# Attention followed by a two-layer MLP: the first two batches as quads of heads, in one written order

## The chip, the cores and the metric

The kernel runs on one core of a Trainium2 chip. The metric is the time of one execution in microseconds (us); a verdict compares the median of several executions of two kernels on the same chip. A profile is of one execution, and its times count from the first instruction of the program (its span).

The engines are PE (TensorE, matrix products, with the weight loads PEld), ACT (ScalarE), DVE (VectorE), POOL (GpSimd) and SP (SyncE). Each works through its own queue in order, and they wait for one another by semaphores. PE writes into PSUM, from where ACT and DVE read. DMAs are issued from the queues of SP, ACT and POOL.

## The reference: what is computed

For each of 8 batches and 12 heads (448 tokens, head size 64):

```python
scores = scale * np.matmul(q, k.transpose(0, 1, 3, 2))
m = np.max(scores, axis=-1, keepdims=True)
e = np.exp(scores - m)
attn = e / (np.sum(e, axis=-1, keepdims=True) + np.exp(-m) + 1e-09)
x = np.matmul(attn, v)          # then [B * S, H * D] = 3584 x 768
h = x @ w_in                    # 768 x 2048
g = np.maximum(h, 0.0) ** 2
out = g @ w_out                 # 2048 x 768
```

The kernel leaves the maximum out: exp(s) / (sum of exp(s) + 1) is the same quotient.

## The kernel before: tiles, stages and the order of the work

**Attention.** Scores are made transposed: keys on the partitions, queries along the columns. So the exponentials (ACT, L222) can go straight into the next product as its moving operand, and the row sums are a product with a tile of ones. The quotient is taken as exp(-ln(sum)) on ACT (L290 and L291), and DVE multiplies it in while it moves the values' product out of PSUM (L299, L302).

Batches 0 and 1 are worked on as *pairs* of heads. `load_natural` puts every fourth token on 112 partitions. `transposes` (L206) makes q and k of two heads of 64 rows each, one above the other. `scores` (L231) then runs two 64 x 112 tiles beside each other on PE (64 rows, 112 columns); `values` (L269) and `row_sums` (L276) run two 112 x 64 tiles. Before the row sums DVE adds the four key chunks up (`add_chunks`, L248).

Batches 2 to 7 are worked on as *quads* of heads: 64 keys at a time, in four 64 x 64 tiles of PE side by side (`visit` L317, `values_quad` L381, `sums_quad` L364). Batch 2 has its q and k transposed on PE (`transposes_quad`, L184); from batch 3 on a DMA does it (`stage`, `transposed_loads`).

**MLP.** `tile_in` (L435) makes 128 of the 2048 hidden features for a stretch of tokens: six products over the 768 inputs, each as two 128 x 64 tiles beside each other (`product`, L419 in mode COLS2). `relu_squared` (L425) takes ReLU and square. `tile_out` (L478) makes 128 tokens x 384 outputs out of 16 products (L491).

**The order.** The instructions of an engine run as they are written. For batch 0 the pairs are units of 192 queries (i = 0 to 5) and then of 256 queries (6 to 11), for batch 1 units of 448 (12 to 17). In the loops from L625 on each unit's scores, sums and values are written with a lag of one or two units, and between them `drain` (L573) puts in as much of the first layer as a share of its estimated time says:

```python
        scores(u, et, 0)
        for at in transpose_at.get(i, ()):
            transposes(*at)
        drain(share[0] * (1.2 if first else 0.45))
        scores(u, et, 1)
        ...
            rcp = row_sums(done, (ess.pop(i - 1)[0:1],))
            values(prev, ets.pop(i - 1), xp)
        drain(share[0] * 0.15)
```

Warm-up matmuls (`keep_warm`, L590) stand at the very start (9) and between the first units (6 more). From L779 on the batches from 2 on run in a steady loop: `between` puts 11 score steps of the quads between products of the second layer or of values, then 16 `tile_in` of the batch before follow, and so on. The first call of `between`, with 11 steps of batch 2 and three `tile_out` of batch 0, comes ahead of the first layer of batch 1.

**Loads** all go through POOL's queue (L520 to L535), in f16, except for the first three pairs of batch 0, which SP and ACT load as they are, in f32, to be cast. Behind batch 0 the queue has half of win, batch 1's first three pairs, the other half of win, batch 1's rest. A load into a buffer that is still read waits for PE.

**PSUM.** `s_psum` has two tiles of [128, 2, 512] for scores, `x_psum` one of [128, 512] and `m_psum` three, for the values, sums, transposes and the MLP. From batch 0's second layer on every fourth such tile is taken from `x_psum`, so that four take turns (`mp_tile`, L403).

Of the kernel before, what the change touches and what calls it, by code (L numbers as in the profile page):

```python
# [16 lines left out]
def kernel(  # L17
# [14 lines left out]
    NPAIR = H // 2  # L32
# [3 lines left out]
    P = S // RUN  # L36
    NQ = H // 4
    KC = S // 64
    PAIRED = (0, 1)
    ON_PE = (0, 1, 2)  # L40
    COLS = H * S // 2 + 16
    HALF = DM // 2

    scale = 1.0 / float(D) ** 0.5
    GS = 256.0
    OUT_SCALE = 1.0 / (GS * GS)

# [14 lines left out]
    x_psum = ctx.enter_context(tc.tile_pool(name="x_psum", bufs=1, space=bass.MemoryType.PSUM))  # L62
    m_psum = ctx.enter_context(tc.tile_pool(name="m_psum", bufs=3, space=bass.MemoryType.PSUM))
# [9 lines left out]
    q_r = q.rearrange("b h (p t) d -> b p h t d", t=RUN)  # L73
    k_r = k.rearrange("b h (p t) d -> b p h t d", t=RUN)
    v_r = v.rearrange("b h (p t) d -> b p h t d", t=RUN)
    win_r = moe_w_in.rearrange("(c p) f -> p c f", p=128)
    wout_r = moe_w_out.rearrange("(c p) f -> p c f", p=128)

    whole, vns, qks, xts, naturals, stages = {}, {}, {}, {}, {}, {}

    def quads_of(t, t0, n, run):

        return t[:, :, t0:t0 + n * run].rearrange("b (i x) (p t) d -> b i p x (t d)", i=2, t=run)

    def load_v_quads(b):
        vn = vns[b] = v_pool.tile([128, NQ, 2, KC, D], FP16, name="vn")
        for i in range(2):
            rows_ = vn[64 * i:64 * i + 64].rearrange("p g j c d -> p (g j) (c d)")
            parts = ((0, KC),) if b in ON_PE else ((0, KC - 1), (KC - 1, KC))
            for c0, c1 in parts:  # L90
                nc.gpsimd.dma_start(out=rows_[:, :, c0 * D:c1 * D], in_=quads_of(v, 64 * c0, 64, c1 - c0)[b, i])

    def load_natural_quads(b, g0, g1):
        t = nat.tile([128, RUN * 2 * S], FP16, name=f"nn{0 if g0 == 0 else 1}")
        w = 2 * S
        for n, r in enumerate((q, k)):
            part = t[:, n * (g1 - g0) * w:(n + 1) * (g1 - g0) * w].rearrange("p (h x) -> p h x", x=S)
            for i in range(2):
                nc.gpsimd.dma_start(out=part[64 * i:64 * i + 64], in_=quads_of(r, 0, 64, KC)[b, i][:, 2 * g0:2 * g1])
            for g in range(g0, g1):  # L100
                naturals["qk"[n], b, "quad", g] = part[:, 2 * (g - g0):2 * (g - g0) + 2].rearrange(
                    "p j (c d) -> p j c d", d=D)

    def load_v(b, p0, p1):
        hs = slice(2 * p0, 2 * p1)
        if b not in vns:
            vns[b] = v_pool.tile([P, H, RUN, D], FP16, name="vn")
        nc.gpsimd.dma_start(out=vns[b][:, hs], in_=v_r[b, :, hs])

    def load_natural(b, p0, p1):  # L110

        raw = b == 0 and p1 <= 3
        for n, r in (("q", q_r), ("k", k_r)):
            src = r[b, :, 2 * p0:2 * p1]
            if raw:
                if p0 == 0:
                    whole[n] = e_pool.tile([P, RUN * S], FP32, name="et")
                t = whole[n][:, p0 * 512:(p0 + 1) * 512].rearrange("p (h t d) -> p h t d", h=2, t=RUN)
                (nc.sync if n == "q" else nc.scalar).dma_start(out=t, in_=src)
            else:  # L120
                if p0 % 3 == 0 and n == "q":
                    whole["both"] = nat.tile([P, RUN * 2 * S], FP16, name=f"nn{p0 // 3}")
                w = NPAIR * RUN * D
                t = whole["both"][:, w * (n == "k"):w * (n == "k") + w].rearrange("p (h t d) -> p h t d", t=RUN, d=D)
                t = t[:, 2 * (p0 % 3):2 * (p0 % 3 + p1 - p0)]
                nc.gpsimd.dma_start(out=t, in_=src)
            for pr in range(p0, p1):
                naturals[n, b, pr] = t[:, 2 * (pr - p0):2 * (pr - p0) + 2]

    def load_win(i, n):  # L130
        w = DF // n
        nc.gpsimd.dma_start(out=win[:, :, i * w:(i + 1) * w], in_=win_r[:, :, i * w:(i + 1) * w])
# [4 lines left out]

# [30 lines left out]

# [13 lines left out]
    def transposes_quad(b, g):  # L184
        if b not in qks:
            qks[b] = qk_pool.tile([128, 3, COLS], FP16, name="qk")
        for n in range(2):
            tp = mp_tile(FP16).rearrange("p a x -> p (a x)")
            for c in range(KC):
                for j in range(2):  # L190
                    nc.tensor.transpose(tp[64 * j:64 * j + 64, 128 * c:128 * c + 128],
                                        naturals["qk"[n], b, "quad", g][:, j, c, :], ident)
            nc.vector.tensor_copy(  # L193
                qks[b][:, n, 2 * S * g:2 * S * (g + 1)].rearrange("p (i c x) -> p c i x", i=2, c=KC),
                tp[:, 0:2 * S].rearrange("p (c i x) -> p c i x", c=KC, i=2))

    def cast(b, pr):
        for name in "qk":
            f = flat.tile([P, 2, RUN, D], FP16, name=f"flat{name}")
            if pr < 2 and name == "k":  # L200
                nc.scalar.activation(out=f, in_=naturals[name, b, pr], func=AF.Copy)
            else:
                nc.vector.tensor_copy(f, naturals[name, b, pr])
            naturals[name, b, pr] = f

    def transposes(b, pr):  # L206
        tp = mp_tile(FP16)
        for i, name in enumerate("qk"):
            for s in range(RUN):
                for h in range(2):  # L210
                    nc.tensor.transpose(tp[64 * h:64 * h + 64, i, P * s:P * s + P],  # L211
                                        naturals[name, b, pr][:, h, s, :], ident[0:P, 0:P])
        if b not in qks:
            qks[b] = qk_pool.tile([128, 3, COLS], FP16, name="qk")
        parts = (0, S // 2, S) if b == 0 and pr < 3 else (0, S)
        for x, y in zip(parts, parts[1:]):
            nc.vector.tensor_copy(qks[b][:, 0:2, pr * S + x:pr * S + y], tp[:, :, x:y])

# [3 lines left out]
    def chunk(et, u, c, kk):  # L224

        n = u[3]
        if n < S:
            return et[:, 0:RUN * 2 * n].rearrange("p (c h j n) -> p c h j n", c=2, h=2, j=2)[:, c, :, kk % 2, :]
        return et.rearrange("p (k x) -> p k x", k=RUN)[:, kk]

    def scores(u, et, c, only=(0, 1)):  # L231
        b, pr, q0, n = u
        qk = qks[b]
        two = [] if n == S else s_psum.tile([P, 2, 512], FP32, name="sp")
        for kk in [2 * c + x for x in only]:
            sp = s_psum.tile([P, 2, 512], FP32, name="sp") if n == S else two
            o = 0 if n == S else kk % 2 * n
            for h in range(2):
                r = slice(64 * h, 64 * h + 64)
# [22 lines left out]
    def of_head(e, u, h):  # L262

        b, _, _, n = u
        if n < S:
            return e[:, h]
# [587 lines left out]
```

## Time and profile before

| | us |
|---|---|
| median of 3 runs | 407.46 (407.33 to 408.98) |
| span of the profiled execution | 405.9 |
| PE busy | 394.9 (97%) |
| DVE busy | 277.2 (68%) |
| ACT busy | 224.1 (55%) |
| first product of batch 1's first layer (L419, 448 columns) starts at | 81.60 |

How to read it: a row of a timeline gives the start, the time from the first start to the last end, the engine, the line, the operation, the tiles written and read, their shape and their number; in brackets the idle time before it and who ended it. Matmuls overlap, so the distance between the starts of two rows says what the first cost. For PE "64*112" are the rows and columns of the array that a matmul uses. In a landing row the last number is the time from issue to landing in us, and KB are those written.

### The profile page before, as it was taken

What the parts mean: (1) busy time and instruction counts of PE and PEld (TensorE: products, weight loads), DVE (VectorE), ACT (ScalarE), POOL (GpSimd) and SP (SyncE); (2) the same over time, 40 slices, a digit from 0 to 9 for tenths busy, and PEclk for the clock granted to TensorE, in tenths of its full rate; (3) what the DMA queues carried; (4) which work ended last, traced back from release to release, by engine and by line L of the source; (5) the groups of instructions that cost most, each with busy time, mean ns of one, the idle gap of its engine ahead of it and who ended that gap; (6) DMA issues with size and microseconds to landing.
All of it is one profiled execution on the core that took longest, in us unless ns stands there. A gap on an engine that the chain in (4) does not pass through costs nothing.

```text
span 405.9 us, 14479 instructions
## 1 busy us (share of the span) xinstructions
PE 394.9 (97%) x6627; PEld 262.4 (65%) x6627; DVE 277.2 (68%) x507; ACT 224.1 (55%) x277; POOL 59.5 (15%) x93
## 2 busy tenths in 40 slices
PE   7899998999999999999999999999999999999997
PEld 3567676667676666757666675757666675555664
DVE  3778888786967867686967867686967868186000
ACT  4898986928465564836466473836466473100111
POOL 6524140005000320003200440005000000000000
PEclk9999999999999999999999999999999999999999
DMA  9999999498706794186925694186501020100222
GB/s 186 197 197 198 203 204 208 105 196 113 175 3 126 122 186 102 42 134 144 189 69 129 119 191 95 42 155 122 120 3 40 3 80 4 48 31 0 79 78 79
DMA packets 77118, 45.83 MB, mean 113 GB/s; under 512 B 46720, under 2 KB 71552, under 8 KB 77056
## 3 DMA queue, kind: packets, MB, share of 16 engines
q0 software_dynamic: 30128, 22.16, 36.5%
q1 hardware_dynamic: 46208, 22.05, 24.5%
q8 instruction: 52, 0.85, 0.9%
q10 hardware_dynamic: 720, 0.69, 0.7%
q14 instruction: 10, 0.08, 0.1%
HBM read 45.69 MB, written 17.93 MB: 157 GB/s over the span
## 4 chain that ended last, share of the span: by engine, by line
PE 87%; DVE 5%; ACT 3%; DMA 2%; issue 1%; ACTq 0%; DVEq 0%
PE mp L491 26%; PE mp L419 22%; PE mp L421 10%; PE xp L419 6%; PE mp L390 6%; PE sp L346 5%; PE xp L421 4%; ACT et L222 2%; DMA et<-in_k_dram 2%; PE sp L241 2%; PE xp L273 2%; PE sp L332 1%; PE mp L211 1%; PE xp L491 1%; PE sp L375 1%
## 5 line engine op out<-in xcount | busy, mean ns | idle before, releaser
L222 ACT ACTIVATE et<-sp 128x896 f16<-128x896 f32 (+3 forms) x132 | 118.0, 915 | 26.0 <-PE sp L346 13.0
L491 PE MATMUL mp<-wout,gs 64*64 64x384 f16 x1760 | 125.6, 323 | 0.0
L419 PEld LDWEIGHTS <-win 128*64 128x64 f16 x1536 | 85.0, 110 | 47.7 <-issue 7.2
L419 PE MATMUL mp<-xt,win 128*64 128x448 f16 (+2 forms) x1248 | 109.0, 324 | 2.2 <-DVE qk L193 1.3
L491 PEld LDWEIGHTS <-gs 64*64 64x64 f16 x2624 | 76.2, 107 | 23.0 <-issue 0.6
L491 PE MATMUL xp<-wout,gs 64*64 64x384 f16 x864 | 84.7, 323 | 0.0
L431 DVE TENSOR_SCALAR rt<-mp 128x448 f16<-128x448 f32 (+2 forms) x82 | 51.0, 622 | 19.0 <-PE mp L419 8.4
L433 DVE TENSOR_TENSOR gs<-rt 128x448 f16<-128x448 f16 (+2 forms) x128 | 50.4, 395 | 12.0 <-ACT rt L429 7.9
L222 ACT ACTIVATE nn<-sp 128x896 f16<-128x896 f32 x42 | 37.6, 913 | 14.0 <-PE sp L346 12.3
L429 ACT ACTIVATE rt<-mp 128x448 f16<-128x448 f32 x18 | 9.8, 543 | 60.0 <-PE mp L419 48.3
L498 DVE TENSOR_SCALAR ot<-mp 128x384 f32<-128x384 f32 x41 | 22.7, 554 | 27.3 <-PE xp L491 19.9
L181 POOL COPY flatq<-qk 64x384 f16<-64x384 f16 x20 | 13.6, 704 | 186.9 <-DMA qk<-stage_k 186.6
L421 PEld LDWEIGHTS <-gs 128*128 128x128 f16 x256 | 24.4, 98 | 15.1 <-issue 0.4
L346 PE MATMUL sp<-qk 64*64 64x224 f16 x720 | 32.9, 258 | 0.0
L419 PE MATMUL xp<-xt,win 128*64 128x448 f16 x288 | 31.3, 352 | 0.0
L421 PE MATMUL mp<-wout,gs 128*128 128x384 f16 (+2 forms) x192 | 29.6, 313 | 0.0
L346 PEld LDWEIGHTS <-qk 64*64 64x64 f16 x720 | 22.4, 119 | 10.7 <-issue 3.6
L500 ACT ACTIVATE ot<-mp 128x384 f32<-128x384 f32 (+2 forms) x12 | 5.6, 463 | 42.4 <-PE mp L421 42.4
L396 DVE TENSOR_TENSOR xt<-mp,rcp 128x448 f16<-128x448 f32 x34 | 19.7, 619 | 8.2 <-PE mp L390 7.8
L378 ACT ACTIVATE rcp<-sp,one_b 128x896 f32<-128x896 f32 x18 | 18.1, 1003 | 6.3 <-PE sp L371 6.3
L390 PEld LDWEIGHTS <-vn 64*64 64x64 f16 x504 | 14.4, 107 | 6.1 <-issue 0.4
L390 PE MATMUL mp<-et,vn 64*64 64x448 f16 x308 | 18.3, 349 | 0.0
(82 smaller groups left out, 392.6 us busy)
## 6 DMA issues: line engine op xcount, KB each, us to landing
out_dram<-ot SPq DMA_DIRECT2D x9, 384.0 KB, 2.3
win<-in_moe_w_in_dram POOLq DMA_DIRECT2D x8, 384.0 KB, 14.0
wout<-in_moe_w_out_dram POOLq DMA_DIRECT2D x4, 768.0 KB, 17.8
vn<-in_v_dram POOLq DMA_DIRECT2D x10, 288.0 KB, 5.4
out_dram<-ot SPq DMA_DIRECT2D x15, 192.0 KB, 3.0
stage_q<-in_q_dram POOLq DMA_DIRECT2D x4, 676.0 KB, 9.8
stage_k<-in_k_dram POOLq DMA_DIRECT2D x4, 676.0 KB, 12.3
out_dram<-ot SPq DMA_DIRECT2D x7, 288.0 KB, 6.0
```

Source lines behind the costliest of these rows:

```text
L181: nc.gpsimd.tensor_copy(km[rows_].rearrange("p h (x o) -> p h x o", o=2)[:, :, :, odd], src[:, :, S // 2 - 32:S // 2])
L222: nc.scalar.activation(out=out_, in_=in_, func=AF.Exp, scale=scale)
L346: nc.tensor.matmul(sp[64 * i:64 * i + 64, o, j * n:(j + 1) * n], keys, qk[r, 0, h * n:(h + 1) * n], start=True, stop=True)
L378: nc.scalar.activation(out=rcp, in_=zp[:, :, 0:S], func=AF.Ln, bias=one_b)
L390: nc.tensor.matmul(xps[i][64 * j:64 * j + 64, 0:S], vns[b][r, g, j, c, :], of_column(e[r], m, j), start=(c == 0), stop=(c == KC - 1))
L396: nc.vector.tensor_mul(xts[b][:, NQ * i + g, :], xps[i][:, 0:S], zqs[m][:, i, :])
L419: nc.tensor.matmul(out_[x:x + 64], lhsT[:, x:x + 64], rhs, start=start, stop=stop)
L421: nc.tensor.matmul(out_, lhsT, rhs, start=start, stop=stop)
L431: nc.vector.tensor_scalar(out=rt[:, 0:m], in0=hp[:, 0:m], scalar1=0.0, scalar2=None, op0=ALU.max)
L433: nc.vector.tensor_mul(gs[:, f0:f0 + per, t0 % RING:t0 % RING + n], r, r)
L491: nc.tensor.matmul(o[y:y + 64, 0:w], g[x:x + 64, y:y + 64], wout[x:x + 64, fb, n0:n0 + w], start=(fb == 0), stop=(fb == NFFB - 1))
L498: nc.vector.tensor_scalar(out=ot[:, n0:n0 + w], in0=op[:, 0:w], scalar1=OUT_SCALE, scalar2=None, op0=ALU.mult)
```

## The change

The pairs and all functions that serve them go (`load_v`, `load_natural`, `cast`, `transposes`, `scores`, `add_chunks`, `values`, `row_sums`, `normalise`, `drain`, `tiles_in_early` and the loops over units). Batches 0 and 1 become quads in 64 x 64 tiles, with 64 partitions for each of two heads. Heads 4g to 4g + 3 are quad g; so win's rows and the order of heads in the later batches change too, without other instructions.

Batch 0 is done in two halves of 224 queries (`half_scores`, `half_exp`). `post` makes values and row sums of a piece together, chunk by chunk on PE, into one pair of PSUM tiles. Half of batch 0's first layer (features 0 to 1023) is made for each half of the tokens (`half_in`), the other half of the features in 64 x 64 tiles over all tokens (`Square`). A square's two PSUM tiles are written by the upper rows of the array and by the lower rows in turn; where they swap, a no-op on SP's queue stands between (`after`).

Everything up to the transposes of batch 2's third quad is in one written order, ORDER, a list of steps. The letters: W warm-up, c cast, t and u transposes and copy of the first quad, T and U those of a quad (b, g, q or k), s scores, e exponentials, p `post`, z and x reciprocal and normalising of a half, i `half_in`, r and g its ReLU and square, q R G the same of a square, a adds, S and Z row sums and reciprocal of a quad, v and X its values and normalising, L loads, P the change of pools, o and O second layer. s, e and p 0 to 23 are pieces of batch 0; s and e 24 to 44 are batch 1's seven chunks of three quads, 45 to 55 those of batch 2. The last number of c, u, r and R says whether ACT does it (1) or DVE (0).

```diff
-    x_psum = ctx.enter_context(tc.tile_pool(name="x_psum", bufs=1, space=bass.MemoryType.PSUM))
-    m_psum = ctx.enter_context(tc.tile_pool(name="m_psum", bufs=3, space=bass.MemoryType.PSUM))
+    begin_psum = ExitStack()
+    x_psum = begin_psum.enter_context(tc.tile_pool(name="x_psum", bufs=1, space=bass.MemoryType.PSUM))
+    m_psum = begin_psum.enter_context(tc.tile_pool(name="m_psum", bufs=2, space=bass.MemoryType.PSUM))
...
+    def xp_pair():
+        return x_psum.tile([128, 2, 512], FP32, name="xp")
...
+    def load_first_quad():
+        raw = e_pool.tile([128, RUN * S], FP32, name="et")[:, 0:2 * S].rearrange("p (n x) -> p n x", n=2)
+        for c0, c1 in ((0, 4 * D), (4 * D, S)):
+            nc.sync.dma_start(out=raw[:, 0, c0:c1], in_=by_pairs["q"][0, :, 0, c0:c1])
+            nc.scalar.dma_start(out=raw[:, 1, c0:c1], in_=by_pairs["k"][0, :, 0, c0:c1])
...
+    def half_scores(at):
...
+        for x in range(2):
+            for o in range(2):
+                if x < len(two[o]):
+                    c, j = two[o][x]
+                    r = slice(64 * j, 64 * j + 64)
+                    for i in range(2):
+                        s0 = (2 * g + i) * S
+                        mm(sp[64 * i:64 * i + 64, o, x * FIRST:(x + 1) * FIRST], qk[r, 1, s0 + 64 * c:s0 + 64 * c + 64],
+                           qk[r, 0, s0 + q0:s0 + q0 + FIRST], start=True, stop=True)
...
+    def post(at):
...
+        for is_sum in range(2):
+            for c, j in todo:
+                for i in range(2):
+                    r = slice(64 * i, 64 * i + 64)
+                    key = (g, half, i, j)
+                    mm(xz[64 * j:64 * j + 64, i, is_sum * FIRST:(is_sum + 1) * FIRST],
+                       ones[r] if is_sum else vns[0][r, j, g, c, :], e[r, j, c], start=key not in opened,
+                       stop=bool(is_sum) and c == KC - 1)
...
+    class Square:
...
+        def part(self, flip, c0, c1):
...
+            for dc in range(c0, c1):
+                self.done += 1
+                for o in range(2):
+                    r = (o + flip) % 2
+                    rows_ = slice(64 * r, 64 * r + 64)
+                    for y in (0, 64):
+                        f = (self.f0 + o) * 128 + y
+                        got = mm(hp[o][y:y + 64, 0:S], win[rows_, dc, f:f + 64], xt[rows_, dc, :],
+                                 start=self.done == 1, stop=self.done == 2 * DCH)
+                        if self.last:
+                            after(got, self.last)
+                            self.last = None
+            if self.done == DCH:
+                self.last = nc.sync.nop()
+                after(self.last, got)
...
-    for pr in range(3):
-        load_natural(0, pr, pr + 1)
+    raw = load_first_quad()
...
-    load_v(0, 0, 3)
-    load_natural(0, 3, 4)
-    load_natural(0, 4, 6)
-    load_v(0, 3, 6)
-    for i in range(4):
-        load_win(i, 8)
-    load_natural(1, 0, 3)
-    for i in range(4, 8):
-        load_win(i, 8)
-    load_natural(1, 3, 6)
-    load_v(1, 0, 6)
+    load_first_second()
+    nat0 = nat.tile([128, RUN * 2 * S], FP16, name="nn0")
+    load_natural_quads(0, (1, 2), 0, nat0)
+    for g in range(NQ):
+        load_v_quads(0, g, g + 1)
+    NW = 4
+    for i in range(NW):
+        load_win(i, NW)
+    load_natural_quads(1, (0,), 0, nat.tile([128, RUN * 2 * S], FP16, name="nn1"))
+    load_v_quads(1)
+    load_natural_quads(1, (1, 2), 0, nat.tile([128, RUN * 2 * S], FP16, name="nn0"))
...
+    def other_ring():
+        begin_psum.close()
+        ring.append(ctx.enter_context(tc.tile_pool(name="ring", bufs=4, space=bass.MemoryType.PSUM)))
...
+    ORDER = """
+        W9 c0,0,0 c1,0,0 t0,0,0 c1,4,1 c0,4,0 t1,0,0 u0,0,0,0 u1,0,0,0 t1,0,4 t0,0,4 u1,0,4,1 s0 u0,0,4,0 t1,1,0
+        u1,1,0,0 t0,1,0 s1 u0,1,0,0 t0,1,4 e0 t1,1,4 u0,1,4,0 e1 u1,1,4,0 s2 T0,1,1 T0,1,0 U0,1,1 s3 T0,2,0 e2
+        e3 U0,1,0 s4 T0,2,1 s5 e4 U0,2,0 p0 s6 p1 e5 e6 s7 e7 p2 p3 U0,2,1 s8 z0 s9 e8 x0 e9 p4 s10 p5 s11 e10
+        p6 p7 s12 e11 z1 e12 s13 x1 p8 s14 e13 p9 e14 s15 e15 p10 p11 s16 s17 z2 x2 e16 p12 s18 p13 e17 e18 s19
+        p14 s20 p15 e19 z3 i0,3 i0,0 x3 r0,3,0 e20 p16 s21 r0,0,1 p17 s22 p18 T1,0,0 g0,3 e21 g0,0 e22 U1,0,0
+        p19 s23 T1,0,1 i0,1 U1,0,1 z4 s24 x4 e23 s25 e24 p20 p21 s26 e25 e26 p22 r0,1,0 s27 p23 z5 T1,1,0 g0,1
+        U1,1,0 i0,2 x5 s28 T1,1,1 r0,2,1 i1,1 e28 U1,1,1 L0 g0,2 e27 i1,0 r1,1,1 s29 r1,0,1 g1,1 s30 T1,2,1 a0,0
+        g1,0 U1,2,1 e29 i1,2 s31 e30 a0,1 a0,2 r1,2,1 s32 g1,2 P0 T2,1,0 e32 e31 a0,3 i1,3 T1,2,0 L1 s33 U2,1,0
+        r1,3,1 U1,2,0 q1,0,0,3 e33 s34 v0,0 g1,3 q1,0,3,6 e34 S0 v0,1 q1,1,0,3 v0,2 s35 v0,3 a1,0 q1,1,3,6 v0,4
+        v0,5 R1,0,0 Z0 s36 e35 R1,1,1 v0,6 G1,0 e36 s37 X0 T2,1,1 T2,0,0 e37 s38 T2,0,1 e38 U2,1,1 s39 q0,0,0,3
+        G1,1 s40 q0,0,3,6 e39 s41 U2,0,1 e40 U2,0,0 v1,0 q0,1,0,3 s42 a1,1 a1,2 e41 v1,1 a1,3 q0,1,3,6 v1,2 S1
+        R0,1,0 e42 v1,3 a2,0 R0,0,1 s43 v1,4 q2,0,0,3 Z1 v1,5 q2,0,3,6 v1,6 X1 s44 e43 G0,1 G0,0 q2,1,0,3 e44
+        s45 q2,1,3,6 e45 R2,0,0 q3,0,0,3 R2,1,1 s46 q3,0,3,6 s47 e46 e47 v2,0 q3,1,0,3 s48 v2,1 G2,1 G2,0
+        q3,1,3,6 v2,2 e48 s49 a2,1 v2,3 R3,0,0 e49 R3,1,0 s50 G3,1 o1,0,4 a2,2 s51 G3,0 a2,3 v2,4 e50 o1,4,8
+        v2,5 e51 s52 a3,0 S2 v2,6 e52 o2,0,4 o1,8,12 o2,4,8 a3,1 o1,12,16 Z2 X2 s53 e53 s54 o2,8,12 o0,0,4 a3,2
+        e54 a3,3 T2,2,0 O1 U2,2,0 S3 s55 o0,4,8 T2,2,1 o0,8,12 o2,12,16 U2,2,1 O2 e55 o0,12,16 Z3 O0
+    """
...
-    for i in range(NPAIR):
-        u, et, es, half = begin(i)
...
     complete(S)
+    del outs[0:EARLY]
...
     for b in range(2, B):
-        m = NQ * (b - 2)
-        n = min(3, len(outs))
-        ns = 12 * PIECE + n * TILE
-        work = second(n)
+        m = NQ * (b - 1)
         if b > 2:
-            ns += KC * PIECE
-            work = chain(timed(values_quad(m - 1)), work)
-        between([(m, c) for c in range(KC)] + [(m + 1, c) for c in range(4)], work, ns, {10: [m]})
-        if b == 2:
-            rcps = row_sums([units[-1]], (ess.pop(len(units) - 1)[0:1],))
-            xp = mp_tile()
-            values(units[-1], ets.pop(len(units) - 1), xp)
-            normalise([units[-1]], xp, rcps)
-            transposes_quad(2, 2)
+            n = min(3, len(outs))
+            ns = 12 * PIECE + n * TILE + KC * PIECE
+            work = chain(timed(values_quad(m - 1)), second(n))
+            between([(m, c) for c in range(KC)] + [(m + 1, c) for c in range(4)], work, ns, {10: [m]})
```

`load_first_second` loads the other two heads of the first quad, `load_natural_quads` q and k of the quads named, `load_v_quads` v, and `load_win` a quarter of win's columns in two DMAs of 64 partitions. L0 in ORDER issues batch 2's first two quads and wout, L1 the third quad, v and the copy of batch 3 for its transposing load.

## The prediction, made before the result was known

> **What bounds the kernel now.** I read the page first, then the window table, then the timelines of PE and ACT up to the place where the two kernels meet again, and last the issues of the loads. The page:
>
> ```profile
> PE 394.9 (97%) x6627; PEld 262.4 (65%) x6627; DVE 277.2 (68%) x507; ACT 224.1 (55%) x277; POOL 59.5 (15%) x93
> ...
> PE   7899998999999999999999999999999999999997
> ...
> ACT  4898986928465564836466473836466473100111
> ```
>
> PE is the bound overall, yet in the first eight slices (about 81 us), where the whole change lies, ACT is nearly as full. By the order of the instructions the two programs meet at the first 448-column matmul of L419 (first layer of batch 1): the last 5388 matmuls have the same shapes in both, with 1239 in front before and 1473 after. So I price only what lies ahead of that matmul, 81.60 us into the span, and keep the 324.3 us behind it.
>
> ```profile
> 0.00:13.30 13.30, 10.46 (x116) 5.22 (x118) 6.62 (x21) 7.45 (x10) 9.58 (x18) 1.00 1.06 188
> 13.30:81.60 68.30, 63.68 (x1125) 45.87 (x1125) 54.38 (x103) 60.13 (x79) 17.18 (x24) 1.00 1.23 187
> 81.60:405.90 324.30, 320.75 (x5388) 211.26 (x5387) 216.19 (x383) 156.55 (x190) 32.71 (x52) 1.00 0.48 94
> ```
>
> (Busy time of PE, PEld, DVE, ACT, POOL; clock; DMA share; GB/s.) In the middle row PE has 63.7 of 68.3 us and ACT 60.1: two engines are close to full. A change here must relieve both, or spread them better.
>
> ```profile
> 1.20 3.59 PE L593 MATMUL mp<-warm 128*128 128x512 f16 x9 [1.20 <-DVE warm L511]
> ...
> 18.09 0.60 PE L593 MATMUL mp<-warm 128*128 128x512 f16 x2
> 18.62 0.43 PE L241 MATMUL sp<-qk 64*112 64x256 f16 x4
> ```
> ```profile
> 50.99 0.58 PE L241 MATMUL sp<-qk 64*112 64x448 f16 x4
> 51.51 0.58 PE L211 MATMUL mp<-ident,nn 112*64 112x112 f16 x16
> 51.93 1.15 PE L419 MATMUL mp<-xt,win 128*64 128x256 f16 x18
> 53.01 0.59 PE L241 MATMUL sp<-qk 64*112 64x448 f16 x4
> ...
> 69.45 0.36 PE L332 MATMUL sp<-qk 64*64 64x448 f16 x4
> 69.64 0.98 PE L491 MATMUL mp<-wout,gs 64*64 64x384 f16 x20
> ...
> 81.60 1.65 PE L419 MATMUL mp<-xt,win 128*64 128x448 f16 x12 [0.64 <-ACT rcp L290]
> ```
>
> PE prices, from start to next start: four 64*64 matmuls of 448 columns run side by side in 0.19 us (69.45 to 69.64), of 224 columns in half of it. Pair scores need two such passes (0.37) but take 0.52 (50.99 to 51.51), and 18 matmuls of 256 columns, nine passes of 0.107, take 1.08 instead of 0.96. So each change between 64-row and 128-row (or 112-row) tiles costs about 0.12 us; L332 to L491, both 64*64, pays nothing. The last line: 0.64 us of waiting for ACT, which ends at this boundary.
>
> ```profile
> 41.34 3.32 ACT L222 ACTIVATE et<-sp 112x896 f16<-112x896 f32 x4
> 44.52 0.66 ACT L290 ACTIVATE rcp<-mp,one_b 128x448 f32<-128x448 f32 x1
> 45.21 0.58 ACT L291 ACTIVATE rcp<-rcp 128x448 f32<-128x448 f32 x1
> ...
> 79.05 1.00 ACT L378 ACTIVATE rcp<-sp,one_b 128x896 f32<-128x896 f32 x1
> 80.08 0.95 ACT L379 ACTIVATE rcp<-rcp 128x896 f32<-128x896 f32 x1
> ```
>
> ACT prices: an exponential of 896 columns every 0.80 us ((3.32 - 0.92) / 3), of 448 about 0.46; a reciprocal of 448 columns 1.19 us (Ln, then Exp 0.69 later, free 0.50 after), of 896 columns 1.88; a ReLU 0.45 (L429, 0.54 less 0.1 overlap).
>
> **The change, part by part.** *PE, removed and added.* By these prices the matmuls ahead of the boundary come to 61 us before (15 warm-up ones among them) and 62 us after. Quads save 12.5% of scores and values, because 112 rows become 128, but batch 0's row sums are now made on PE chunk by chunk (24 "p" steps of twice the values' passes, 3.9 us more than a values pass alone) and the adds of batch 0 leave DVE. What shrinks is the number of changes of tile form: 73 before, 38 after, 35 x 0.12 = 4.2 us. *ACT* keeps its work: 60 to 62 us. *DVE* comes to 42 us ahead of the boundary and is in no stretch above both others.
>
> *Sum by stretches of the written order,* PE (changes of form included) against ACT; the larger counts, because scores have only two tiles in PSUM, so PE can lead ACT by two exponentials at most:
>
> - s6 to s20: 14 scores, 14 p: PE 8.0; 12 exponentials of 896, 2 of 448, 3 reciprocals: ACT 13.75.
> - s20 to s24: 3 i steps (1.14 each), 2 T (0.41), 5 p, 4 s, 5 changes: PE 7.0; ACT 5.7.
> - s24 to s31: 4 i, 3 T, 4 p, 7 s, 6 changes: PE 9.2; ACT 7.8.
> - s31 to s38: PE 8.3; 8 exponentials, 3 ReLUs, 1 Z: ACT 9.6.
> - s38 to s42: PE 3.4; ACT 2.4.
> - s42 to s48: PE 7.1; 7 exponentials, 2 ReLUs, 1 Z: ACT 8.4.
> - s48 to the end: 48 of the "o" passes (0.16), 6 v, 8 s, 2 S, 2 T, 3 q passes, 9 changes: PE 13.1; ACT 10.2, DVE 11.5.
>
> The larger ones sum to 64.5 us.
>
> *The start, up to s6.* The first "p" waits for batch 0's v of quad 0, which stands behind q and k of all quads on POOL's queue; s6 stands behind that p on PE. Landings before (issue plus time to landing): 1456 KB by 12.5 us, 1680 KB by 13.7, if raw f32 is counted as the half that it would be in f16. After, 1568 KB go ahead: 13.1 us. If raw f32 costs by bytes written, it is 11.2. I take 12.7, and 0.8 for p0: s6 at **13.5**. The first scores come earlier than now (half the bytes ahead of them) but the second step, t1,1,0, waits for POOL's first load, so nothing is gained there.
>
> *Batch 1's first quad.* Loads are moved: all of win (3072 KB) now goes ahead of batch 1's q and k, before only half.
>
> ```profile
> 12.27 0.78 POOL L126 DMA_DIRECT2D nn<-in_q_dram  x1
> ```
> ```profile
> nn<-in_q_dram POOLq DMA_DIRECT2D x1, 336.0 KB, 13.6
> ```
>
> So they landed at 25.9 us and were used at 30.5. After, 5312 KB stand ahead or are it: by the win landings before (5376 KB at 33.9) 33.6 us, by bytes written 30.4. PE reaches T1,0,0 at 13.5 + 13.75 + 4.4 - 0.8 = 30.9. Behind it on PE stand p19, s23, i0,1 and s24, and so ACT from the second exponential on. Wait 0 to 2.7 us; I take **1.5**.
>
> *New waits.* Each of four squares passes its accumulation from one row half to the other through SP: the last matmul's 0.35 us and two hops stand against two passes (0.37) written in between. 0 to 0.5 us each, by nothing waiting and by the whole matmul uncovered; I take 0.1, **0.4** in all. The 4-tile ring starts behind the last x and ReLU of the old pools, just ahead of T2,1,0; T2,1,0's own data, issued after T1,0,1, need about 10 us (8.9 before for a like load) and arrive about when it is due: 0 to 1 us, taken as nothing. SP's queue has four no-ops ahead of the first store, which is at 78 us now: nothing.
>
> *What is absorbed.* Where a PE-bound stretch follows an ACT-bound one (at s20, s38, s48) ACT still has two exponentials in hand, so PE's excess is partly free: 0 to 1.6 us each; I take one exponential, 3 x 0.80 = **2.4**.
>
> Boundary: 13.5 + 64.5 + 1.5 + 0.4 - 2.4 = 77.5, 4.1 us ahead of 81.6. Span 405.9 - 4.1 = 401.8; the median of the runs lies 1.6 above the profiled span, so **403.4 us**.
>
> *A rule against the change.* The nine first warm-up matmuls take 0.40 us each, the two at 18.09 about 0.21: TensorE begins slow, though the clock column reads 1.00 throughout. The change drops six later warm-up matmuls from a start that is thin anyway. The Trainium skill ("TensorE: Matmul & The Clock Gate", section "Part 1: The HAM clock gate") says that an idle window of about 3.4 us halves the clock again. No wait that I find between 4.4 and 13.5 us is that long, so I add nothing; by that rule one such window would cost about 1.7 us.
>
> **The rivals.**
>
> 1. *Nothing absorbed, loads late (no gain).* ACT and PE take turns, each idle while the other works, and batch 1 lands by the later estimate: 77.5 + 2.4 + 1.2 = 81.1, 407.0 us. For it: the order has stretches with 5.7 us more ACT than PE, and the new PE sum is hardly smaller. Against: in the stretches behind s31 the sums differ by only 15 to 25%.
> 2. *Better overlap.* No wait at T1,0,0 and the whole PE excess of s20, s24, s38 and s48 (1.3, 1.4, 1.0, 1.6) hidden: 13.5 + 64.5 - 5.3 = 72.7, 398.6 us. ACT's own sum behind s6, 57.8, allows no less than 71.3, which is 397.2.
> 3. *Slower: win blocks batch 1.* Its pieces now have 64 rows; if these move at two thirds of the rate (3072 KB in 23 instead of 15.4 us), T1,0,0 waits 7.7 us more: boundary 85.2, 411.1 us. It decides the sign from 4.1 us more of lateness. Against: 64-row loads of L99, issued 0.6 us apart, landed 1.1 us and 224 KB apart, the same 200 KB per us.
>
> **How the numbers follow.** Forecast (boundary 76 to 79.5) 0.57; better 0.17; no gain 0.19; slower 0.07. 0.5% of the time, 2 us, is about what a measurement here can tell from no change: faster 0.74, same 0.19, slower 0.07. The range takes in most of both neighbours: 398.3 to 408.0.
>
> **What would show it.** In the new profile: the first 448-column matmul of the plain first layer at about 77.5 us; ACT without gaps from 13.5 to 27 us while PE idles; a PE wait of about 1.5 us for batch 1's q near 31 us; no change-of-form cost between scores, values and squares; DVE never the releaser for long. I am wrong if ACT has gaps of its own between s6 and s20 (waits of p for x0, x1, ...), if the wait at T1,0,0 is above 3 us, or if the part behind the boundary is not 324 us long.

## The result, and the profile after

| | before | after |
|---|---|---|
| median of 6 runs each | 408.40 | 406.84 (406.01 to 407.19) |
| ratio, 95% interval | | 0.9964 (0.9947 to 0.998) |
| span of the profiled execution | 405.87 | 405.40 (that run: 407.19) |
| boundary (batch 1's first 448-column product) | 81.60 | 80.59 |
| from there to the end | 324.26 | 324.81 |

The forecast was 403.4 us, a gain of 4.1; measured are 1.6 us, and between the two profiles 0.5. The time is inside the range, the size of the gain is not what was forecast. The page of the changed kernel:

```profile
PE 392.2 (97%) x6861; PEld 260.8 (64%) x6861; DVE 258.9 (64%) x466; ACT 222.0 (55%) x279; POOL 60.1 (15%) x95
...
PE   8878999999999999999999999999999999999996
...
ACT  4897899718375565827475564827366473100111
...
q8 instruction: 53, 0.87, 0.9%
```

PE is busy 2.7 us less, but with 234 matmuls more. The last line, which I had not read before the prediction, is the queue that brings instructions: 53 packets of 16 KB, 256 instructions of 64 bytes each. PE alone has 2 x 6861 = 13,722 instructions (each matmul has its weight load), 53.6 such blocks. The stretches (busy PE, PEld, DVE, ACT, POOL; clock; DMA share; GB/s), cut at s6 and at the boundary:

```profile
0.00:13.77 13.77, 11.82 (x154) 6.98 (x157) 6.41 (x20) 7.27 (x11) 10.64 (x21) 1.00 0.99 162
13.77:80.59 66.82, 59.87 (x1328) 43.47 (x1322) 37.35 (x65) 58.65 (x80) 16.33 (x23) 1.00 1.10 181
80.59:405.40 324.81, 320.55 (x5392) 210.31 (x5386) 215.10 (x382) 156.07 (x189) 33.18 (x52) 1.00 0.48 96
```

s6 starts at 13.77, as forecast (13.5). From there to the boundary 64.0 us were forecast (64.5 + 1.5 + 0.4 - 2.4); it took 66.82, with PE idle for 7 us of them. PE's waits up to the boundary, by releaser (total, times, longest):

```profile
PE xp L95 <- DVE xt L328: 4.4, 3, 1.6
...
PE mp L95 <- issue: 0.9, 2, 0.7
PE mp L206 <- issue: 0.7, 1, 0.7
PE mp L206 <- DMA nn<-in_k_dram: 0.4, 2, 0.3
```

The first is the wait of p4, p8 and p12 for the one pair of PSUM tiles; ACT is busy beside it, as forecast. The second and third have no releaser in the profile. Before, PE had no such gap in this profile. The rows of the changed kernel at two of the places (start, duration, operation; in brackets the idle time before):

```profile
33.76 0.30 PE L206 MATMUL mp<-ident,nn 128*64 128x128 f16 x3 [0.15 <-DMA nn<-in_k_dram]
34.74 0.49 PE L206 MATMUL mp<-ident,nn 128*64 128x128 f16 x11 [0.69 <-issue]
35.05 1.34 PE L95 MATMUL mp<-xt,win 128*64 128x224 f16 x24
```
```profile
39.45 0.55 PE L95 MATMUL mp<-xt,win 128*64 128x224 f16 x7
40.67 1.02 PE L95 MATMUL mp<-xt,win 128*64 128x224 f16 x17 [0.67 <-issue]
```

PE stops in the middle of a step, after 3 of 14 transposes and after 7 of 24 products, where nothing is left to wait for. Counted from PE's first instruction, the gaps (a third at 53.32, 0.24 us; one more at 287.59) stand ahead of number 1218, 1476, 1987 and 10947: all 194 to 196 behind a multiple of 256 (counted in the order of the starts). So I take that place for the end of a block, and read the times from the trace:

| PE enters a block | the 16 KB packet that starts next | PE enters the next block | of it a gap |
|---|---|---|---|
| after: 29.05 | 32.26 to 33.20 | 34.80 | 0.69 |
| 34.80 | 38.44 to 39.42 | 40.76 | 0.67 |
| 40.76 | 44.37 to 45.34 | 46.91 | |
| 46.91 | 50.84 to 51.80 | 53.33 | 0.24 |
| 53.33 | 57.01 to 57.90 | 59.52 | |
| before: 35.87 | 38.86 to 39.80 | 44.64 | |
| 44.64 | 46.78 to 47.72 | 53.01 | |
| 53.01 | 55.34 to 56.31 | 61.57 | |

After, the packet starts 3.2 to 3.9 us behind the entry, and PE goes on 1.3 to 1.6 us behind its end: about 6 us for 256 instructions in these five blocks. Before, the three blocks shown last over 8 us, since fewer and wider matmuls stand in them, and the next is there in time. The 6 us are no floor: in the changed kernel the block from 18.06 to 23.13 took 5.07 us (its packet started 1.8 us behind the entry), and before, the one from 29.70 to 35.87 took 6.17, both without a gap and with loads of about 200 GB/s.

Theory **F** (fetch): while the loads keep the DMA queues full, PE gets a block of 256 instructions every 6 us or so over a run of blocks, and the changed kernel, with 1473 matmuls ahead of the boundary for 1239, runs into that between 29 and 66 us. Theory **T** (taking turns, the forecast's first rival): nothing of PE's excess is absorbed by ACT, and the gaps belong to their steps.

### The profile page after: what moved, and what is told of

It is laid out like the page before. It is cut to its first block, busy times and chain, and to the rows that moved or that the text cites. A ratio compares the mean times of both kernels' runs of the same rounds, so it can differ in the third digit from the quotient of the medians.

```text
span 405.4 us, 14903 instructions
## 1 busy us (share of the span) xinstructions
PE 392.2 (97%) x6861; PEld 260.8 (64%) x6861; DVE 258.9 (64%) x466; ACT 222.0 (55%) x279; POOL 60.1 (15%) x95
## 4 chain that ended last, share of the span: by engine, by line
PE 86%; DMA 6%; ACT 2%; DVE 2%; POOL 2%; issue 1%; POOLq 0%; DVEq 0%
PE mp L95 76%; PE sp L95 9%; DMA nn<-in_k_dram 3%; DMA win<-in_moe_w_in_dram 3%; PE mp L206 1%; ACT et L245 1%; POOL nn L124 1%; POOL vn L112 1%; ACT rt L472 0%; DVE gs L478 0%; DVE rt L474 0%; DVE xt L441 0%; DVE half L392 0%; DVE half L390 0%; ACT rcp L416 0%
## 5 line engine op out<-in xcount | busy, mean ns | idle before, releaser
L95 PE MATMUL mp<-wout,gs 64*64 64x384 f16 (+3 forms) x2784 | 164.3, 322 | 0.7 <-issue 0.7
L95 PE MATMUL mp<-xt,win 128*64 128x448 f16 (+3 forms) x1632 | 154.1, 342 | 0.7 <-issue 0.7
L95 PEld LDWEIGHTS <-win 128*64 128x64 f16 (+2 forms) x1632 | 90.1, 109 | 57.6 <-issue 4.9
L245 ACT ACTIVATE et<-sp 128x896 f16<-128x896 f32 (+1 forms) x131 | 112.9, 889 | 23.9 <-PE sp L95 20.3
L95 PEld LDWEIGHTS <-gs 64*64 64x64 f16 (+2 forms) x2784 | 100.1, 106 | 39.6 <-issue 3.2
L474 DVE TENSOR_SCALAR rt<-mp 128x448 f16<-128x448 f32 x95 | 59.1, 623 | 19.3 <-PE mp L95 16.0
L472 ACT ACTIVATE rt<-mp 128x448 f16<-128x448 f32 x33 | 18.0, 545 | 78.7 <-PE mp L95 66.9
L95 PE MATMUL sp<-qk 64*64 64x224 f16 (+1 forms) x1056 | 58.4, 274 | 0.6 <-ACT et L245 0.3
L478 DVE TENSOR_TENSOR gs<-rt 128x448 f16<-128x448 f16 x128 | 50.0, 392 | 13.0 <-ACT rt L472 9.2
L187 POOL COPY flatq<-qk 64x384 f16<-64x384 f16 x20 | 14.1, 725 | 193.0 <-DMA qk<-stage_k 192.7
L441 DVE TENSOR_TENSOR xt<-mp,rcp 128x448 f16<-128x448 f32 x42 | 24.2, 619 | 10.5 <-PE mp L95 8.6
L578 DVE SCALAR_TENSOR_TENSOR ot<-mp,ot 128x384 f32<-128x384 f32 x38 | 21.2, 558 | 4.0
L416 ACT ACTIVATE rcp<-rcp 128x896 f32<-128x896 f32 x21 | 20.0, 951 | 0.7
L392 DVE TENSOR_TENSOR half<-half,et 128x1792 f16<-128x1792 f16 x15 | 16.7, 1110 | 0.1
## 6 DMA issues: line engine op xcount, KB each, us to landing
stage_k<-in_k_dram POOLq DMA_DIRECT2D x4, 676.0 KB, 13.6
```

The source lines that it names most:

```text
L95: return nc.tensor.matmul(out_, lhsT, rhs, start=start, stop=stop)
L245: nc.scalar.activation(out=out_, in_=in_, func=AF.Exp, scale=scale)
L392: nc.vector.tensor_add(esq[m], esq[m], z[:, 0:w])
L416: nc.scalar.activation(out=rcp, in_=rcp, func=AF.Exp, scale=-1.0)
L441: nc.vector.tensor_mul(xts[b][:, 2 * g + i, :], xqs[m][i][:, 0:S], zqs[m][:, i, :])
L472: nc.scalar.activation(out=rt[:, 0:m], in_=hp[:, 0:m], func=AF.Relu)
```

## The experiments

Times are medians; the ratio is to the kernel before on the same chip. "p4 to boundary" is from the profile, and leaves the start out, which differs by execution. "Gaps" are PE's idle times with releaser "issue" ahead of the boundary.

| | us | ratio (95%) | s6 | p4 to boundary | gaps |
|---|---|---|---|---|---|
| changed kernel | 406.84 | 0.9964 (0.9947 to 0.998) | 13.8 | 62.6 | 0.69, 0.67, 0.24 |
| e2_noops | 407.01 | 0.9955 (0.9919 to 0.9991) | 14.2 | 62.6 | 0.09, 0.67, 0.24 |
| after_again | 407.00 | 0.9971 (0.9954 to 0.9987) | 15.5 | 62.3 | 0.76, 0.67, 0.16 |
| e3_full | 405.60 | 0.9957 (0.9928 to 0.9986) | 16.0 | 60.6 | none |
| e4_order | 408.02 | 0.9988 (0.9957 to 1.0019) | 14.7 | 62.1 | 0.84, 0.67, 0.25 |
| e5_light | 405.29 | 0.9943 (0.9925 to 0.996) | 13.3 | 60.9 | 0.76 |
| e6_split | 408.58 | 1.0033 (1.001 to 1.0056) | 17.4 | 62.3 | 0.75 |
| e7_zdve | 424.24 | 1.0397 (1.0371 to 1.0423) | 13.6 | 77.6 | none |
| b3_three | 424.78 | 1.0419 (1.0397 to 1.0441) | 13.2 | 78.5 | none |
| e8_tmove | 407.46 | 0.9979 (0.996 to 0.9997) | 13.5 | 62.9 | 1.21, 1.66, 1.08 |
| b4_full_tmove | 405.86 | 0.9948 (0.9929 to 0.9967) | 15.8 | 60.6 | 0.73, 1.10 |
| e9_ln | 406.88 | 0.9974 (0.9952 to 0.9996) | 16.0 | 61.7 | 0.33, 1.39, 0.12, 0.16 |
| b6_fewer | 403.46 | 0.9879 (0.9854 to 0.9904) | 13.8 | 60.3 | none |
| b7_later | 402.58 | 0.9864 (0.984 to 0.9889) | 14.5 | 59.3 | 0.13 |

**e2_noops.** `nc.tensor.nop()` 32 times ahead of p8 and of p12.

> Adds 64 PE no-ops, 32 ahead of p8 and 32 ahead of p12, where PE waits 1.4 us anyway. Theory F: the blocks of 256 instructions end 64 instructions earlier in the order, so the 'issue' gaps move to other steps, and PE, which between 29 and 66 us gets a block every 6.0 us, comes up to 64/256 x 6.0 = 1.5 us later to the boundary: 81.5 to 82.1. Theory T: the no-ops vanish in the waits; gaps at the same steps (T1,0,1, i0,2, v), boundary 80.6.

The no-ops are not in the compiled program (PE has its 13,722 instructions), so this is a repeat of the changed kernel: the gaps stand at the same places again, which tells nothing between F and T. One thing differs. At T1,0,1 PE waited 1.00 us for batch 1's k, and only 0.09 us of the gap there is left: late data and late instructions hide each other.

```profile
34.82 0.88 PE L206 MATMUL mp<-ident,nn 128*64 128x128 f16 x14 [1.00 <-DMA nn<-in_k_dram]
```

**e3_full.** In `half_in`:

```diff
+        mode[0] = FULL
         if c0 == 0:
...
+        mode[0] = COLS2
```

> The eight i steps (batch 0's first layer by halves) use 128x128 tiles instead of two of 128x64: 96 matmuls and so 192 PE instructions fewer, with the same passes. Theory F: three quarters of a block less to fetch between 28 and 60 us, so the gaps of 2.1 us go: boundary about 78.5. Theory T: PE's passes are the same, so 80.6, or later if the wider weight loads show.

60.6 us from p4 on, 2.0 less, as F says, and no gap is left. T had no gain here. The passes are the same, only the number of instructions is not: 12 matmuls of an i step take 1.32 us (at 36.09), as 24 narrower ones took 1.34 (at 35.05 in the changed kernel). In the whole time it is not clear of noise: 405.60 us against 407.01 in e2_noops on the same chip, with nearly the same ratio to the kernel before. What PE waited for up to the boundary, whole:

```profile
PE xp L95 <- DVE xt L328: 4.4, 3, 1.6
PE mp L206 <- DMA nn<-in_k_dram: 2.1, 1, 2.1
PE xp L95 <- DVE warm L602: 1.2, 1, 1.2
PE sp L95 <- ACT et L245: 0.6, 3, 0.3
PE mp L232 <- DVE qk L242: 0.3, 1, 0.3
```

The second row is why this profile's boundary stays at 80.87: here the first loads came 2 us late.

**e4_order.** `load_win(2, 4)` and `load_win(3, 4)` behind batch 1's loads.

> The second half of win is loaded behind batch 1 instead of ahead of it. Both theories: the 0.26 us of waiting for batch 1's q and k at 32.6 and 33.8 go. Theory F: as many bytes are under way, so the blocks come no sooner and the 'issue' gaps stay: boundary 80.3 to 80.6 (PE that comes earlier to a block's end only waits longer for it). Theory T: 80.3. If the forecast's price of the load order (1.5 us) were right, 79.1.

The waits for batch 1's data go (0.26 us), the gap at T1,0,1 grows from 0.69 to 0.84. In no run here was the load order worth the forecast's 1.5 us (1.0 in e2_noops).

**e5_light.**

```diff
-    wout = persist.tile([128, NFFB, DM], FP16, name="wout")
+    unused = persist.tile([128, NFFB, DM], FP16, name="wout")
+    wout = win[:, :, 0:DM]
...
-                        f = (self.f0 + o) * 128 + y
+                        f = (self.f0 + o) % 8 * 128 + y
...
-    for i in range(NW):
+    for i in range(NW // 2):
...
-        for n0 in (0, HALF):
-            for y in range(2):
-                load_wout(n0, y, 2)
```

> Leaves out the loads of wout and of the second half of win (the first half of win stands in for both, so the products have other values and the same shapes). Theory F (instruction fetch): PE takes its instructions in blocks of 256; with the load queues full the 16 KB packet of the next block starts 3.6 us after PE entered a block, and the block is usable 1.3 to 1.6 us behind the packet's end, so PE gets a block every 6.0 us at most. Without these loads the packets start sooner (below 3 us), the 'issue' gaps ahead of the boundary go, and the time from p4 to the boundary (62.6 us in the changed kernel) falls by 2.1 of stalls and 0.26 of waiting for batch 1's data, to about 60.2 us. Theory T (PE and ACT take turns, the gaps belong to their steps): 62.3 us.

Mostly as F says: 60.9 us. Behind PE's entry at 34.05 the next packet now starts 1.05 us later instead of 3.64 (the DMAs moved 8 GB/s from 34 to 36 us, 204 in the changed kernel), and the gaps at i0,2 and v are gone. The gap at T1,0,1 stays: PE entered the block before it at 28.6 us, when batch 1's loads were still under way, and the packet started 3.05 us later.

**e6_split.**

```diff
-                    mm(xz[64 * j:64 * j + 64, i, is_sum * FIRST:(is_sum + 1) * FIRST],
+                    parts = (0, 112, 224) if is_sum and 4 <= at < 12 else (0, 224)
+                    for y0, y1 in zip(parts, parts[1:]):
+                        mm(xz[64 * j:64 * j + 64, i, is_sum * FIRST + y0:is_sum * FIRST + y1],
...
```

> The row sum products of p4 to p11 are written as two halves of 112 columns each: 56 matmuls and so 112 PE instructions more for the same columns, in the stretch where PE waits for ACT and DVE. Theory F: from block 5 on PE gets a block every 6.0 us, and the 112 instructions more cost up to 112/256 x 6.0 = 2.6 us: p4 to the boundary 64 to 65.2 us (62.6 in the changed kernel), with the 'issue' gaps at other steps. Theory T: they hide in the waits of s6 to s20, 62.6 us with the gaps at the same steps.

Neither number. The median is slower than before, 1.7 us above the changed kernel's, and the gaps of T1,0,1, i0,2 and v are gone, with a new one in the sums of a p at 31.7 us: against T. But F's 64 us were not reached: this execution began 3.6 us later, and by the time it came to the later blocks the loads were further on (71 to 101 GB/s from 39 to 43 us; packets 2.1 to 3.0 us behind the entry). Its 62.3 us are also no clean measure: the granted clock was 0.50 from 31.34 to 34.76 us, and p4 to T1,0,0 took 16.7 us, 14.4 in e5_light, of which the gap is 0.75.

**e7_zdve and b3_three.** In `half_z`, b3_three together with the edits of e3_full and e4_order:

```diff
-        nc.scalar.activation(out=rcp, in_=xz[:, :, FIRST:2 * FIRST], func=AF.Ln, bias=one_b)
-        nc.scalar.activation(out=rcp, in_=rcp, func=AF.Exp, scale=-1.0)
+        nc.vector.tensor_scalar(out=rcp, in0=xz[:, :, FIRST:2 * FIRST], scalar1=1.0 / GS, scalar2=None, op0=ALU.add)
+        nc.vector.reciprocal(rcp, rcp)
```

> The six reciprocals of batch 0's halves are made on DVE (add 1/256, then reciprocal) in place of Ln and Exp on ACT. If ACT sets s6 to s20, as the forecast's sum has it, that stretch falls by 3 x 1.19 = 3.6 us from 14.3 to about 10.7, less what the DVE operations keep p4, p8 and p12 waiting. Theory F: behind it PE waits for batch 1's q and k, which land at 32.6 as before, so the boundary gains only the stall at 34.7, about 0.9 us: 79.7. Theory T: nothing limits PE but ACT and the data, boundary 79 to 80.3.

> Three edits together: the i steps in 128x128 tiles (192 PE instructions fewer), the second half of win behind batch 1's loads, batch 0's reciprocals on DVE. Theory F: no stall for instructions (2.1), no wait for batch 1's data (0.3), s6 to s20 shorter by 3.6: p4 to the boundary about 57.5 us in place of 62.6, boundary 75 if the first loads land as in the changed kernel, time 401 to 402. Theory T: the i steps gain nothing, boundary 77.

Both far off: I had priced DVE's reciprocal like its other operations. The group (line, operation, shapes, count, then busy and mean ns of one) in e7_zdve:

```profile
L322 DVE RECIPROCAL rcp<-rcp 128x448 f32<-128x448 f32 x6 | 17.7, 2954 | 0.2
...
L328 DVE TENSOR_TENSOR xt<-xp,rcp 128x448 f16<-128x448 f32 x6 | 3.7, 623 | 0.2
```

2.95 us, nearly five times a multiplication of the same shape, and p4, p8 and p12 wait for it 4 us each, two later steps 1.0 and 3.2 us. These waits (16.0 us for 4.4) are not all of the 15 us that e7_zdve lost: the granted clock was 0.50 behind them, in 17 of the 77.6 us, and in 24 of b3_three's 78.5. One such stretch (the clock is the third number from the end):

```profile
34.70:41.40 6.70, 5.67 (x98) 5.21 (x100) 2.76 (x4) 2.38 (x3) 0.00 (x0) 0.50 0.97 156
```

The two say nothing on F and T.

**e8_tmove and b4_full_tmove.** Loads in the order nn1 (batch 1's first two quads), half of win, v, batch 1's third quad, half of win; in ORDER:

```diff
- ... s13 x1 p8 ...
+ ... s13 T1,0,0 T1,0,1 x1 U1,0,0 U1,0,1 p8 ...
...
- ... s16 s17 z2 x2 e16 p12 ...
+ ... s16 s17 z2 T1,1,0 T1,1,1 x2 U1,1,0 U1,1,1 e16 p12 ...
```

(These steps go from their later places.)

b4_full_tmove has the edit of e3_full as well.

> Batch 1's first two quads are loaded ahead of win, the second half of win last, and their four transposes (T1,0,0, T1,0,1, T1,1,0, T1,1,1) move up to where PE waits for x1 and x2. By sums without fetching this takes 4 x 0.41 us and some changes of tile form, 2.4 us, out of stretches in which PE is the bound: p4 to the boundary 60.0 - 2.4 = 57.6 us. Theory F (a block of 256 PE instructions costs 6.0 us while the loads run; the number of instructions is as before): most of it is lost in stalls ahead of s31, 59.5 to 61.5 us. Theory T: 62.5 - 2.4 = 60.1 us with the stalls at i0,2 and v as before.

> The same, and the i steps in 128x128 tiles (192 PE instructions fewer). Theory F: at most one short stall (below 0.7 us) near the end of block 4; p4 to the boundary 58.2 to 59 us (60.6 in the run with the 128x128 i steps alone, less 2.4), so 2 us faster than that run and 3.5 to 4 us faster than the changed kernel: 402.5 to 403.5. Theory T: the i steps give nothing, as e8_tmove.

The clearest of all against T: by the sum 2.4 us of PE's work moved into waits, and nothing gained, 62.9 us. PE's waits up to the boundary in e8_tmove:

```profile
PE xp L95 <- issue: 4.0, 3, 1.7
PE xp L95 <- DVE xt L328: 2.6, 3, 1.6
```

What the waits for x lost (4.4 to 2.6), those for instructions gained. From the entry of block 3 to that of block 10 it took 43.8 us, 42.8 in the changed kernel: 6.1 to 6.3 a block. F's size was too small (59.5 to 61.5): I had left blocks 3 and 4 out, where packets started 3.5 and 4.1 us late. The same holds for b4_full_tmove, 60.6 for 58.2 to 59.

**e9_ln.** The Exp in `half_z` left out.

> Leaves out the second step (Exp) of batch 0's six reciprocals, so that batch 0 is scaled with the logarithm; ACT has 0.52 us less for each. If ACT sets s6 to s20, as the forecast's sum has it, the stretch falls by 3 x 0.52 = 1.6 us from 14.1 to 12.5. If PE's waits for x (1.4 to 1.6 us each) set it through the single pair of PSUM tiles, it also falls by up to 1.6, but ACT then shows idle time in s6 to s20; by the forecast it has none beyond the 0.4 us ahead of z0 and e6.

s6 to s20 took 13.31 us for 14.08, half of the 1.6. From p4 on ACT has no idle time, and p4 to s20 falls by 1.21 for two shorter reciprocals (1.04): ACT does set that part. Ahead of p4 this execution lost 0.4 us at half clock (below). To the boundary only 0.6 of it is left (61.7 us, 62.3 in after_again on the same chip): the gaps grow to 2.0 us.

**b6_fewer and b7_later.** b4_full_tmove with additions on DVE ahead of the row sums (steps A in ORDER):

```diff
+    def add_half(at):
+        g, half, k = HALVES[at]
+        e = half_e(g, half)
+        s = added[at] = es_pool.tile([128, 4 * S], FP16, name="half")[:, 0:2 * FIRST].rearrange("p (j n) -> p j n", j=2)
+        nc.vector.tensor_add(s, e[:, :, 2 * k], e[:, :, 2 * k + 1])
```

and then, in b7_later, T2,1,0 from behind P0 to behind s33, and "i0,0 i0,3" for "i0,3 i0,0".

> b4_full_tmove, and in front of the row sums of batch 0 (all but its first half quad) DVE adds two chunks into one, so that 60 row sum matmuls and with them 120 PE instructions go; DVE has 15 additions of about 0.4 us more, PE less than 3 us less, all of it in stretches where b4_full_tmove stood at the ends of blocks 4 and 5 for 0.73 and 1.10 us. Theory F: these two gaps go, the time from p4 to the boundary falls from 60.6 to 58.8 to 59.4 us, and the time by as much, to about 404.5. If the gaps were not those of fetching, PE would find other waits (ACT is as busy as before) and it stays at 60.6.

> b6_fewer, with T2,1,0 three steps later (behind s33) and i0,0 ahead of i0,3. If the order of the steps is the reason, both waits (0.55 us for win's second quarter, 1.08 us for batch 2's q) go and nothing takes their place: p4 to the boundary 58.7 to 59.1 us in place of 60.3, time about 402.3. If the loads' rate sets the stretch, PE waits for the same data at the later places and it stays above 59.8 us.

In b6_fewer the gaps are gone, as F says, but p4 to the boundary is 60.3: waits for win (0.55) and batch 2's q (1.08) came in their place. By that number the other case (60.6) is as near. The time fell by 2.4 us all the same. Between the two profiles it is 3.9: 0.3 between p4 and the boundary, and the rest (start 2.0, behind the boundary 1.7) in parts that differ from execution to execution, so one profile of each can't say whose it is. b7_later settles the two waits: it was the order of the steps, they go and little takes their place (59.3 us, 0.2 above what was expected). PE's waits up to the boundary:

```profile
PE xp L95 <- DVE xt L343: 2.6, 3, 1.6
PE xp L95 <- DVE warm L617: 1.2, 1, 1.2
PE sp L95 <- ACT et L245: 1.0, 3, 0.5
PE mp L232 <- DMA flatk<-in_k_dram: 0.6, 1, 0.6
PE xp L95 <- DMA vn<-in_v_dram: 0.2, 1, 0.2
```

402.58 us, 1.4% less than before, beats both kernels (the intervals of the ratios are apart), and lies below the forecast's 403.4: with 156 matmuls fewer than the changed kernel, and with other loads and steps earlier or later.

**after_again, before_again.** Both kernels once more.

> The changed kernel once more, for the comparison on the same chip. Both theories: 406 to 407.5 us; the stretches behind p4 as in its first profile within 0.3 us, and s6 anywhere from 13.2 to 17.4 us, as the first loads land.

> The kernel before once more. If stalls for instructions behind the boundary come by execution, this profile has one or two 'issue' gaps on PE (0.3 to 1 us) behind 80 us, and the part behind the boundary is 324.0 to 325.5 us long. If they belong to the changed kernel alone, there is none and the part is 324.2 to 324.4 us long. Ahead of the boundary no 'issue' gap in either case, since a block lasts 7.3 us or more there. The first products wait for the first loads 0 to 2.5 us longer or shorter than in the first profile.

The changed kernel has its gaps at T1,0,1 and i0,2 again, the third a block earlier (48.5 us). The kernel before (407.79 us, ratio 0.9991, 0.9975 to 1.0006) again has none ahead of its boundary, at 81.01 (though one block there lasts only 6.16 us, 29.10 to 35.26, for the 7.3 or more expected), but this time one behind it:

```profile
PE mp L491 <- issue: 1.2, 1, 1.2
```

and 325.31 us from the boundary on. So stalls there come by execution in both kernels (0 to 1.6 us over the profiles here). Whether the changed kernel has them more often, two profiles of the kernel before can't tell.

## Why the prediction was wrong, point by point

The stretches of the written order, in us; "unstalled" is the shortest of the runs in which the same steps ran without a gap (e5_light; T1,0,0 to s24 from e6_split):

| | forecast | after | unstalled |
|---|---|---|---|
| start to s6 | 13.5 | 13.8 | |
| s6 to s20 | 13.75 | 14.1 | 14.1 |
| s20 to s24 | 7.0 + 1.5 - 0.8 | 8.5 | 7.2 |
| s24 to s31 | 9.2 | 10.6 | 9.7 |
| s31 to s38 | 9.6 | 9.1 | 9.0 |
| s38 to s42 | 3.4 - 0.8 | 3.5 | 3.4 |
| s42 to s48 | 8.4 | 7.7 | 7.6 |
| s48 to the end | 13.1 - 0.8 | 13.3 | 13.3 |

- **The step that failed** is the price of PE's work, "the matmuls ahead of the boundary come to 61 us before (15 warm-up ones among them) and 62 us after". It counts passes and changes of tile form. The prediction had the other number in hand, 1239 matmuls and 1473, and made no term of it. The stalls cost 1.0 us at T1,0,1, 0.9 at i0,2 and 0.4 in the three stretches behind, 2.3 in all: the durations after less those unstalled (at T1,0,1 also less 0.26 of waiting for data). e3_full, with the same passes and fewer instructions, gives 2.0 back between p4 and the boundary; that is shown.
- *"What is absorbed", 2.4 us at s20, s38 and s48:* wrong in place and size. There PE's sum is paid in full (7.2, 3.4, 13.3). Instead the stretches that ACT should set are shorter than its sum: 9.0 for 9.6 and 7.6 for 8.4, 1.4 us.
- *The wait for batch 1's first quad, 1.5 us:* 0.11 and 0.15 (1.0 in e2_noops). *The hand-overs, 0.4 us:* no gap on PE. Both too dear, and by luck they hide the error of absorption: unstalled, s6 to the boundary takes 64.2 us, against 64.0 forecast.
- *s6 to s20 with ACT as its bound:* right (ACT idles 0.46 us ahead of e6 and 0.39 ahead of z0, not from p4 on). The price is 0.3 too low by a slip: the counts given there make 12 x 0.80 + 2 x 0.46 + 3 x 1.19 = 14.1, not 13.75.
- *The start:* 13.8 for 13.5 in the first profile, in part luck, since the other runs have s6 at 13.2 to 17.4. *T2,1,0, taken as nothing:* 0.13 us, and that for a ReLU on ACT (L472), not for its data. *The part behind the boundary:* 324.8 for 324.3, with a gap of 0.73 in it.
- *The rivals.* The first, 407.0 us, is nearest to the time, but not by its mechanism: 1.4 us were absorbed and the loads were in time. The conditions under "I am wrong if" did not warn of it, since none was about instructions.

The Trainium skill has the mechanism, which the prediction did not draw on: "Runtime: NRT & Kernel Launch", section "Instruction fetch mechanics", says that an engine's instructions are refilled in 16 KiB blocks of 256 by a DMA queue of its own, and that crossing a block is "mostly hidden". The packets here agree with the block; that it is hidden holds for the kernel before ahead of its boundary, not for 2.3 us of the changed one and 4.0 of e8_tmove.

What stays open: why a packet starts 3 to 4 us late beside the loads. e5_light shows that the loads have a part in it, but their rate alone does not set it: at about 200 GB/s packets also started 1.8 us (changed kernel, entry 18.06) and 2.0 to 2.9 us (e3_full, entries 32.13 to 58.18) behind the entry. Open too is whether smaller loads would let it pass, which was not tried.

## What to carry to other kernels

Count a stretch's instructions beside its passes: a kernel made of small tiles can be short of instructions while every engine has room, above all where bulk loads run. The sign is an idle time of PE without a releaser in the middle of a step, at distances that are multiples of 256 instructions. The cure here was the same work in fewer matmuls (128x128 tiles for two of 128x64, additions on an idle engine ahead of row sums) before a better order: moving work earlier gained nothing by itself (e8_tmove), and reordering gained 1.0 us only when the gaps were gone (b7_later).

## What the runs showed of the hardware

- Where the gaps stand, a block of 256 PE instructions took 5.7 to 6.4 us in the changed kernel (29.05 to 65.97) and 5.9 to 6.6 in e8_tmove (22.20 to 66.01), while the loads moved some 205 GB/s. Single blocks beside the same loads took 5.07 (changed kernel, from 18.06) and 5.24 us (e3_full, from 32.13).
- DVE's reciprocal took 6.6 ns per column (2954 ns for 448), its multiplication 1.4 (623 ns).
- The granted clock fell where the first loads were late. In after_again PE waited 1.84 us for batch 0's k at 8.7 to 10.5 us, and then (the clock is the third number from the end):

```profile
8.00:10.00 2.00, 0.70 (x11) 0.37 (x9) 0.60 (x2) 1.39 (x3) 0.70 (x2) 1.00 1.07 148
10.00:12.00 2.00, 1.46 (x30) 1.29 (x30) 0.62 (x1) 0.00 (x0) 1.03 (x3) 0.70 1.25 200
12.00:14.00 2.00, 2.00 (x30) 1.24 (x28) 0.95 (x2) 0.79 (x2) 1.25 (x2) 0.50 1.27 205
14.00:16.00 2.00, 2.00 (x54) 1.83 (x52) 0.93 (x2) 1.78 (x2) 0.90 (x2) 0.95 1.25 206
```

28 transposes took 1.51 us instead of 0.97, and from their start to p0 it was 4.31 us instead of 3.39 (14.85 - 10.54, 13.14 - 9.75). The price is 0.9 us. The same wait was 1.59 to 2.56 us in the other profiles whose clock fell to 0.50 there (e9_ln, b4_full_tmove, e3_full, e6_split), and 1.14 us in e4_order, whose clock stayed at 1.00. A wait's length alone does not decide: 1.6 us ahead of p4 lowered the clock in no profile. The rule of the clock gate that the prediction weighed and set aside ("TensorE: Matmul & The Clock Gate", section "Part 1: The HAM clock gate") asks for an idle window of about 3.4 us. Here shorter waits were enough, and the price is about half of the 1.7 us by the rule. It is no part of the miss: the first profile has a clock of 1.00 throughout, and the other five runs behind the median have a mean of 0.999 or more.
